# A fused attention, DFT and FFN kernel on one core: contiguous output of the first DFT stage, conversion of the second weight matrix over more slots, the first layer norm in one go, FFN at slot 37

## The chip, the cores and the metric

The kernel runs on one core of a Trainium2 chip. The metric is the time of one execution on the device in microseconds (us), as the median of several runs. A core has five engines with instruction queues of their own: TensorE (PE; its weight loads are listed as PEld), VectorE (DVE), ScalarE (ACT), GpSimd (POOL) and SyncE (SP), which here issues every DMA. Each queue runs strictly in the order in which it was written.

## The reference

```python
# attention: 8 batches, 8 heads, 512 local + 32 global tokens, head dim 64
s_ll = where(|pos_i - pos_j| <= 32, q_l @ k_l.T / 8, -1e9)
out_l = sm([q_l @ k_g.T / 8, s_ll]) @ [v_g, v_l]      # local rows: a band and the globals
out_g = sm(q_g @ [k_g, k_l].T / 8) @ [v_g, v_l]       # global rows: all keys
# x: (8, 544, 512)
mixed = real(fft(fft(x, axis=1), axis=2))
u  = x + mixed
un = (u - mean(u)) / sqrt(var(u) + 1e-6)
return u + relu(un @ w_ch1) @ w_ch2                   # 512 -> 2048 -> 512
```

The weights come as 64-bit numbers and are converted on the chip. Operands of matmuls are split into a float16 high part and a float16 low part, and each product is three matmuls: high by high, high by low, low by high.

## The kernel before, in words

`Kern.run` writes a plan: every call of a step is entered with a time, and `Plan.run` calls them in order of that time. So the plan's times are nothing but an order; each engine's queue is the order of the calls that use it. Up to time 38 (`F0`) one unit is a slot, and an attention step for 128 query rows (a "tile" u) goes in each slot; `A[u]` is u for the first 16 tiles and u + 6 afterwards (`PAUSE`: six slots without a new tile after batch 0). From `F0` on the FFN runs beside the attention: `warp` stretches the plan so that 22 slots take 32 units (two FFN chunks), and after that 2 units go to a slot.

**Attention.** Per pair of heads p: loads, scales, products by the scales, high and low parts (`prep_*`, `v_*`), then per two tiles `scores` (PE), `masked` (DVE, L409), `exps` (ACT, L418), and per tile `p_hi` (ACT, L422), `p_lo` (POOL, L426), a transposing DMA `turn`, `values` (PE, L444 and L446), and `norm` (DVE, L455 to L457). `x_out` writes the rows to a DRAM buffer `xs`; the next pair's first `norm` writes the same one-buffer tile `x`. `g_*` are the same for the global rows (`g_values`, L499). `scales` is a run of small DVE steps on two or four values a partition (L312 to L329).

**Weights.** For each of 32 tiles of 128x512 there is a load (`w_load`, 512 KB), `w_abs` (ACT, L183, into one of two PSUM buffers named ps1), and `w_bits` (four DVE passes, L191 to L194), in this order: 16 tiles of w_ch1 (k = 0), then 16 of w_ch2 (k = 1). Tile n has its `w_bits` in slot n - 8, so w_ch2 takes slots 8 to 23, one tile each. Then `w_max`, `w_fold` and `w_scale` find the scale, and `w_split` makes the two parts: for w_ch2 two ACT passes (L249, L258) and one POOL subtraction (L259). All 16 of these stand in slots 26 to 33, two to a slot. Raw tiles lie in two buffers `rw`, which share their place with the DFT's input `x4`, and in two buffers `raw`, which share theirs with the FFN's transposed input `uh`.

**DFT of a batch**, from slot R + 7 with R the batch's last tile's slot: `d_load` reads `xs`, `d_odd*` (POOL, L593 and on), `d_tail` and `d_even*` (DVE, L597 to L609 and L643 to L648) fold it, `d_hi` and `d_lo` split it. Then come five `d_first` (PE, L676 and L678; 8 matmuls of 137 columns each, the two halves of the 274 columns written to even and odd columns of a PSUM tile), each followed by `d_z` (ACT, L685) and `d_z2` (DVE, L690), which take its high and low part out of PSUM; and six `d_second` (PE, L700, 129 columns each) with `d_as`, `d_df` and `d_add`. Two steps go in a slot. Batch 0 takes its PSUM from the two buffers ps1, later ones from a single buffer psd.

**FFN**, 17 chunks of 256 rows. A chunk's layer norm (`l_stats`, `l_un`, `l_hi`, `l_lo`, `l_turn`, `l_root`; L753 to L789) starts 6 units before the chunk, 5 for chunks 0 and 1. Then for each of 8 pairs fp of blocks: `f_first` (PE, L801, 24 matmuls), `f_hi` (ACT, L806), `f_lo` (DVE, L810), and 3 units later `f_second` (PE, L820, 12 matmuls), which reads the w_ch2 tiles 2 fp and 2 fp + 1. `f_end` and `f_out` close the chunk.

Of the kernel before, what the change touches and what calls it, by code (L numbers as in the profile page):

```python
# [10 lines left out]
F16 = mybir.dt.float16  # L11
BF16 = mybir.dt.bfloat16
I32 = mybir.dt.int32
AF = mybir.ActivationFunctionType
ALU = mybir.AluOpType
# [4 lines left out]
P = 128  # L20
B, H, SL, SG, D = 8, 8, 512, 32, 64
T, DM, FF = 544, 512, 2048
NK, NL, NH = 274, 258, 129
# [4 lines left out]
NVB = 2  # L28
NKB = 2
W0 = -8  # L30
F0 = 38
PAUSE = 6
RS0 = 1.829591166069289e-20

# [40 lines left out]
class Plan:  # L75
# [3 lines left out]
    def add(self, slot, rank, fn, *a):  # L79
        self.at(self.warp(slot + rank), fn, *a)  # L80

    def at(self, time, fn, *a):
        self.q.append((time, len(self.q), fn, a))
# [6 lines left out]
class Kern:  # L90
    def __init__(self, tc, stack, ins, out):
# [57 lines left out]
        self.g, self.st, self.w, self.cur = {}, {}, {}, {}  # L149
        self.u, self.dsc, self.D, self.L, self.raw = {}, {}, {}, {}, {}  # L150

# [13 lines left out]
        return self.wd[1][i * P:(i + 1) * P, :]  # L165

    def w_load(self, k, i, n):
        if n % 4 < 2:
            if n == 0:
                rw = self.p1.tile([P, 2, 512, 2], I32, name="rw", tag="x4")  # L170
                self.rw = [rw[:, j] for j in range(2)]
            raw = self.rw[n % 2]
        else:
            raw = self.p2.tile([P, 512, 2], I32, name="raw", tag="uh")
        self.nc.sync.dma_start(raw.rearrange("p n t -> p (n t)"), self.w_src(k, i).bitcast(I32))
        self.raw[k, i] = raw
# [487 lines left out]
    def d_first(self, b, i):  # L664
        nc, d = self.nc, self.D[b]
        eh, ht = d["eh"], d["ht"]
        cs, o, d0, m = (*divmod(i, 2), 0, P) if i < 4 else (0, 0, P, 1)
        d["ps"] = ps = self.d_psum(b)[:m, 0:NK]
        base = (0, 258, 514, 770)[2 * cs + o]
        w = 128 + (base == 0)  # L670
        n = NK // 2
        for kp in (1, 0):
            c0, po = n - n * kp, ps[:, 1 - kp:NK:2]
            for k, (a, c) in enumerate(((0, 0), (0, 1), (1, 0))):
                e = base + kp * w + d0
                nc.tensor.matmul(po, eh[:, a, e:e + m], self.c1[:, cs, c, c0:c0 + n], start=k == 0, stop=False)  # L676
            e = (0, 129, 257, 385)[2 * cs + o] + d0
            nc.tensor.matmul(po, ht[:, e:e + m], self.c1t[:, cs, c0:c0 + n], start=False, stop=True)  # L678

    def d_z(self, b, i):  # L680
        d = self.D[b]
        if i < 4 and i % 2 == 0:
            d["z", i // 2] = self.p1.tile([P, 2, 2, NK], F16, name=f"z{i // 2}")
        d["hl"] = (d["z", i // 2][:, 0, i % 2], d["z", i // 2][:, 1, i % 2]) if i < 4 else (self.zr[0:1, :], self.zr[32:33, :])
        self.nc.scalar.activation(d["hl"][0], d["ps"], AF.Copy, scale=0.125)  # L685

    def d_z2(self, b, i):
        d = self.D[b]
        hi, lo = d.pop("hl")
        self.nc.vector.scalar_tensor_tensor(lo, d.pop("ps"), 0.125, hi, op0=ALU.mult, op1=ALU.subtract)  # L690

    def d_second(self, b, kt, cs):
        nc, d = self.nc, self.D[b]
# [50 lines left out]
    def l_stats(self, c):  # L744
# [3 lines left out]
        v, y = ve[:, 0], ve[:, 1]  # L748
        self.L[c] = {"mv": mv, "ve": ve, "uh": None}
        for j in range(2):  # L750
# [8 lines left out]
    def l_un(self, c, j):  # L759
        L = self.L[c]  # L760
        L["un"] = un = self.p1.tile([P, DM], F32, name="un", tag="un")
        self.nc.vector.tensor_scalar(un, self.u[c][:, j], L["mv"][:, j, 0:1], L["ve"][:, 1, j:j + 1], op0=ALU.subtract, op1=ALU.mult)  # L762

    def l_hi(self, c, j):
        L = self.L[c]
        L["hl"] = hl = self.p2.tile([P, 2, DM], F16, name="unh")
        self.nc.scalar.activation(hl[:, 0], L["un"], AF.Copy)  # L767

    def l_lo(self, c, j):
        L = self.L[c]  # L770
        self.nc.vector.tensor_sub(L["hl"][:, 1], L.pop("un"), L["hl"][:, 0])

    def l_turn(self, c, j):
        L = self.L[c]
        if j == 0:
            L["uh"] = self.p2.tile([P, 2, 8, P], F16, name="uh", tag="uh")
        self.nc.sync.dma_start_transpose(L["uh"][:, j], L.pop("hl").rearrange("p a d -> p (a d)"))

    def l_root(self, c):
        nc = self.nc  # L780
# [55 lines left out]
    def run(self):  # L836
        self.h = {}
        late = F0 + 16 + PAUSE

        def warp(t):  # L840
            if t < F0:
                return t
            return F0 + 32 * (t - F0) / (16 + PAUSE) if t < late else F0 + 32 + 2 * (t - late)

        plan = Plan(warp)
        add, at = plan.add, plan.at
# [3 lines left out]
        for n in range(32):  # L850
            k, t = divmod(n, 16)
            i = t if k else 4 * (t % 4) + t // 4
            s = W0 + n
            add(s - 3, .08, self.w_load, k, i, n)
            add(s - 1, .71, self.w_abs, k, i)
            add(s, .40, self.w_bits, k, i)
            if n % 4 == 3 and k == 0:
                c = n // 4
                add(s, .41, self.w_max, 0, c)
                add(s + 1, .62, self.w_fold)  # L860
                add(s + 2, .62, self.w_scale, 0, c)
                for kt in range(4):
                    add(s + 3 + kt, .75, self.w_split, 0, 4 * kt + c)
        s = W0 + 31
        add(s, .41, self.w_max, 1, 0)
        add(s + 1, .62, self.w_fold)
        add(s + 2, .62, self.w_scale, 1, 0)
        for f in range(16):
            add(s + 3 + f // 2, .75, self.w_split, 1, f)
        add(8, .09, self.load_consts)  # L870

        for b in range(B):
# [7 lines left out]
        for p in range(32):  # L880
# [19 lines left out]
            for half in range(2):  # L900
                t = A[4 * p + 2 * half]
# [21 lines left out]
        for b in range(B):  # L923
# [17 lines left out]
            for n, e in enumerate(steps):  # L941
                t, r = R + 14 + n // 2, (.50, .52, .56) if n % 2 == 0 else (.90, .92, .94)
# [13 lines left out]
            add(t + 2, .07, self.d_rest, b)  # L956
        at(F0 + 32 * 7 + 4.5, self.l_load)
        for c in range(17):
            F = F0 + 16 * c
            L = F - (6 if c > 1 else 5)  # L960
            at(L + .42, self.l_stats, c)
            for j in range(2):
                at(L + j + 1.425, self.l_un, c, j)
                at(L + j + 1.76, self.l_hi, c, j)
                at(L + j + 1.79, self.l_lo, c, j)
                at(L + j + 2.03, self.l_turn, c, j)
            at(L + 3.43, self.l_root, c)
            for fp in range(8):
                t = F + 2 * fp
                at(t + .30, self.f_first, c, fp)  # L970
                at(t + .54, self.f_hi, c, fp)
                at(t + .65, self.f_lo, c, fp)
                at(t + 3.30, self.f_second, c, fp)
            for j in range(2):
                at(F + 17.82, self.f_end, c, j)
            at(F + 18.04, self.f_out, c)
# [52 lines left out]
```

## Time and profile before

| | us |
|---|---|
| median of three runs | 1208.02 |
| the three runs | 1207.30, 1208.02, 1210.46 |
| the profiled execution | 1210.44 |
| its span, first to last instruction | 1208.7 |
| mean granted TensorE clock in it | 0.966 |
| first FFN matmul starts | 245.3 |

Times in views of the trace count from the first instruction. A row of busy times by stretch reads: stretch, its length, then for PE, PEld, DVE, ACT and POOL the busy time in it (and the instructions), then the granted clock, the DMA engines' busy share and GB/s. A row of the chain of waits reads: start, length, engine, tile, line, number of instructions in a row; it follows the work that ended last back to what released it. A group row reads: busy time, mean ns of one | idle time before it.

### The profile page before, as it was taken

What the parts mean: (1) busy time and instruction counts of PE and PEld (TensorE: products, weight loads), DVE (VectorE), ACT (ScalarE), POOL (GpSimd) and SP (SyncE); (2) the same over time, 40 slices, a digit from 0 to 9 for tenths busy, and PEclk for the clock granted to TensorE, in tenths of its full rate; (3) what the DMA queues carried; (4) which work ended last, traced back from release to release, by engine and by line L of the source; (5) the groups of instructions that cost most, each with busy time, mean ns of one, the idle gap of its engine ahead of it and who ended that gap; (6) DMA issues with size and microseconds to landing.
All of it is one profiled execution on the core that took longest, in us unless ns stands there. A gap on an engine that the chain in (4) does not pass through costs nothing.

```text
span 1208.7 us, 24459 instructions
## 1 busy us (share of the span) xinstructions
PE 1011.3 (84%) x9415; PEld 728.0 (60%) x9415; DVE 761.5 (63%) x2121; ACT 608.6 (50%) x1348; POOL 505.6 (42%) x473
## 2 busy tenths in 40 slices
PE   0244325499798999999999999999999999999996
PEld 0234224366575667766777677767677767666664
DVE  6998873856857575767576747674867446433221
ACT  4667569666565555665565556555554212111110
POOL 2779177745544534453446344634462311100000
PEclk9999998589898999999999999999999999999998
DMA  7669925556455645464556546644444221110000
GB/s 250 151 171 234 268 65 111 124 124 166 104 141 98 157 99 133 99 160 110 120 114 150 113 114 122 143 114 104 108 110 103 66 85 36 38 56 18 27 27 18
DMA packets 249564, 137.55 MB, mean 114 GB/s; under 512 B 200576, under 2 KB 223200, under 8 KB 249448
## 3 DMA queue, kind: packets, MB, share of 16 engines
q1 hardware_dynamic: 249448, 136.01, 46.5%
q8 instruction: 73, 1.20, 0.4%
q14 instruction: 43, 0.35, 0.1%
HBM read 65.10 MB, written 18.35 MB: 69 GB/s over the span
## 4 chain that ended last, share of the span: by engine, by line
PE 63%; DVE 24%; ACT 7%; POOL 2%; issue 2%; DMA 2%; DVEq 0%; ACTq 0%; POOLq 0%
PE acc L820 25%; PE ps L801 25%; PE S L399 3%; DVE pe L409 2%; PE psd L676 2%; PE bk L499 2%; DVE ps L192 2%; DVE ps L193 2%; DVE ps L191 2%; DVE wm L194 1%; PE psd L700 1%; PE bk L444 1%; PE bk L446 1%; DVE h L810 1%; ACT pe L418 1%
## 5 line engine op out<-in xcount | busy, mean ns | idle before, releaser
L801 PE MATMUL ps<-uh,wh 128*128 128x256 f16 x3264 | 383.2, 274 | 0.0
L820 PE MATMUL acc<-wh,h 128*128 128x512 f16 x1632 | 380.8, 384 | 0.0
L801 PEld LDWEIGHTS <-wh 128*128 128x128 f16 x3264 | 320.2, 99 | 59.6 <-issue 0.8
L810 DVE SCALAR_TENSOR_TENSOR h<-ps,h 128x512 f16<-128x512 f32 x136 | 93.7, 689 | 303.4 <-ACT h L806 303.3
L820 PEld LDWEIGHTS <-h 128*128 128x128 f16 x1632 | 154.8, 99 | 172.8 <-issue 11.5
L426 POOL TENSOR_TENSOR ph<-pe,ph 128x448 f16<-128x448 f32 x128 | 134.6, 1052 | 292.8 <-ACT ph L422 116.8
L806 ACT ACTIVATE h<-ps 128x512 f16<-128x512 f32 x136 | 80.3, 590 | 258.3 <-PE ps L801 258.1
L418 ACT ACTIVATE pe<-pe,nm 128x224 f32<-128x224 f32 x256 | 102.1, 470 | 97.9 <-DVE nm L409 97.7
L444 PE MATMUL bk<-vN,pl 128*128 128x65 f16 x768 | 74.3, 205 | 68.4 <-DVE xg L509 35.0
L409 DVE CUSTOM_DVE_ANT_0 pe<-S,msk,z 128x224 f32<-128x224 f32 x256 | 99.6, 445 | 3.1 <-PE S L399 3.1
L446 PEld LDWEIGHTS <-pl 96*128 96x128 f16 x768 | 61.5, 106 | 52.2 <-issue 50.9
L444 PEld LDWEIGHTS <-pl 128*128 128x128 f16 x768 | 64.3, 106 | 26.4 <-DMA pl<-ph 20.3
L399 PE MATMUL S<-kT,qT 64*128 64x192 f16 x768 | 57.5, 277 | 18.8 <-ACT pg L480 18.5
L422 ACT ACTIVATE ph<-pe 128x448 f16<-128x448 f32 x128 | 72.0, 563 | 0.0
L399 PEld LDWEIGHTS <-qT 64*128 64x128 f16 x1536 | 55.4, 103 | 22.5 <-issue 19.0
L377 POOL TENSOR_TENSOR kT<-qk,kT 128x512 f16<-128x512 f32 x32 | 40.8, 1274 | 53.3 <-ACT kT L372 51.4
L767 ACT ACTIVATE unh<-un 128x512 f16<-128x512 f32 x34 | 21.3, 625 | 75.4 <-DVE un L762 75.4
L446 PE MATMUL bk<-vB,pl 96*128 96x65 f16 x576 | 55.7, 205 | 0.0
L362 ACT ACTIVATE qk<-qk,z 128x512 f32<-128x512 f32 x64 | 45.5, 710 | 15.5 <-DVE z L323 15.5
L352 POOL TENSOR_TENSOR vN<-vf,vN 128x640 f16<-128x640 f32 x32 | 46.2, 1444 | 0.3 <-ACT vN L348 0.3
L593 POOL TENSOR_TENSOR s<-x 128x1020 f32<-128x1020 f32 x8 | 19.1, 2382 | 57.7 <-DMA x<-xs 30.7
L377 POOL TENSOR_TENSOR qT<-qk,qT 128x512 f16<-128x512 f32 x32 | 38.6, 1207 | 9.9 <-DMA u<-xs 6.6
(185 smaller groups left out, 1663.2 us busy)
## 6 DMA issues: line engine op xcount, KB each, us to landing
qk<-in_qk SPq DMA_DIRECT2D x32, 512.0 KB
vf<-in_v SPq DMA_DIRECT2D x32, 320.0 KB
rw<-in_moe_w_ch SPq DMA_DIRECT2D x16, 512.0 KB
raw<-in_moe_w_ch SPq DMA_DIRECT2D x16, 512.0 KB
xs<-x SPq DMA_DIRECT2D x32, 256.0 KB
out<-u SPq DMA_DIRECT2D x16, 512.0 KB
x<-xs SPq DMA_DIRECT2D x24, 256.0 KB
u<-xs SPq DMA_DIRECT2D x24, 256.0 KB
```

Of the source, the lines that this page charges most:

```text
L377: self.nc.gpsimd.tensor_sub(lo, s.pop(nm), hi)
L399: nc.tensor.matmul(ps, qT[r, a, j], k, start=m == 0, stop=m == 2)
L409: nc.vector.tensor_tensor_reduce(self.per[(4 * p + j) % 4][:, h, 0:224], S[:, h, 224 * n:224 * n + 224], self.msk[:, j], z[:, 8:9], 3e38, ...
L418: nc.scalar.activation(pe[:, h, 0:224], pe[:, h, 0:224], AF.Exp, bias=nm[:, n, h:h + 1], scale=-1.0)
L422: self.nc.scalar.activation(ph[:, 0, :, 0:224], self.per[i % 4][:, :, 0:224], AF.Copy)
L426: self.nc.gpsimd.tensor_sub(ph[:, 1, :, 0:224], self.per[i % 4][:, :, 0:224], ph[:, 0, :, 0:224])
L444: nc.tensor.matmul(pv[:, j % 2, h], pl[:, 4 * a + 2 * h], vN[:, j, c, h, :], start=m == 0, stop=False)
L446: nc.tensor.matmul(pv[:, j % 2, h], pl[0:96, 4 * a + 2 * h + 1], vb, start=False, stop=m == 2)
L801: nc.tensor.matmul(ps[:, q], wt[:, w, c0:c0 + P], uh[:, :, 4 * a + kt, :], start=n == 0, stop=n == 11)
L806: self.nc.scalar.activation(h[:, 0], self.fps, AF.Relu)
L810: self.nc.vector.scalar_tensor_tensor(h[:, 1], self.fps, 0.0, h[:, 0], op0=ALU.max, op1=ALU.subtract)
L820: nc.tensor.matmul(self.acc_f[j], h[:, a, q, j * P:(j + 1) * P], self.w[1, f][:, w, :], start=f == 0 and a == 0 and w == 0, stop=f == 15 a ...
```

## The change

Five edits.

1. `d_first` writes its two halves side by side in PSUM. `d_z` and `d_z2` read the halves as they lie and write their float16 results to every second column, so that the tiles read by `d_second` are as before.
2. The w_ch2 tile t has its `w_bits` in slot 8 + (3t // 2) where it was 8 + t: 8, 9, 11, 12, 14, 15, 17, 18, 20, 21, 23, 24, 26, 27, 29, 30. Its load and `w_abs` stay three slots and one slot ahead. `w_max`, `w_fold` and `w_scale` follow in slots 30 to 32.
3. `w_split` of w_ch2 goes to slots 33 to 48, one each (at .75), where it was 26 to 33, two each.
4. The tiles from n = 24 on no longer use `rw`: every third of them uses a new buffer `rx`, the others `raw`.
5. `F0` is 37. Chunk 0's norm is started at F0 - 4 with its halves close together (times 33.42 to 34.10, root at 36.43); it was spread over 33.42 to 36.43. Chunk 1's norm starts 6 units ahead as the later ones do (5 before). The high and low tile `hl` of a half is kept under the half's own key, since both halves are now in flight.

```diff
-F0 = 38
+F0 = 37
...
-        if n % 4 < 2:
+        if n > 23 and n % 3 == 2:
+            raw = self.p1.tile([P, 512, 2], I32, name="rx")
+        elif n < 24 and n % 4 < 2:
...
-            c0, po = n - n * kp, ps[:, 1 - kp:NK:2]
+            c0 = n - n * kp
+            po = ps[:, c0:c0 + n]
...
-        self.nc.scalar.activation(d["hl"][0], d["ps"], AF.Copy, scale=0.125)
+        self.nc.scalar.activation(self.woven(d["hl"][0]), self.halves(d["ps"]), AF.Copy, scale=0.125)
+
+    def woven(self, t):
+        return t.rearrange("p (k o) -> p o k", o=2)
+
+    def halves(self, t):
+        return t.rearrange("p (o k) -> p o k", o=2)
...
-        self.nc.vector.scalar_tensor_tensor(lo, d.pop("ps"), 0.125, hi, op0=ALU.mult, op1=ALU.subtract)
+        self.nc.vector.scalar_tensor_tensor(self.woven(lo), self.halves(d.pop("ps")), 0.125, self.woven(hi), op0=ALU.mult, op1=ALU.subtract)
...
-            s = W0 + n
+            s = W0 + (n if k == 0 else 16 + 3 * t // 2)
...
-        s = W0 + 31
...
-            add(s + 3 + f // 2, .75, self.w_split, 1, f)
+            add(s + 3 + f, .75, self.w_split, 1, f)
...
-            L = F - (6 if c > 1 else 5)
+            if c == 0:
+                L, x, y, z = F - 4, (.50, .60), (.02, .06), (.30, .50)
+            else:
+                L, x, y, z = F - 6, (1.425, 2.425), (.335, .365), (.605, .605)
             at(L + .42, self.l_stats, c)
             for j in range(2):
-                at(L + j + 1.425, self.l_un, c, j)
-                at(L + j + 1.76, self.l_hi, c, j)
-                at(L + j + 1.79, self.l_lo, c, j)
-                at(L + j + 2.03, self.l_turn, c, j)
+                at(L + x[j], self.l_un, c, j)
+                at(L + x[j] + y[0], self.l_hi, c, j)
+                at(L + x[j] + y[1], self.l_lo, c, j)
+                at(L + x[j] + z[j], self.l_turn, c, j)
```

More of the change, by code (lines that the diff above doesn't have):

```diff
@@ L765, in l_hi @@
         L = self.L[c]
-        L["hl"] = hl = self.p2.tile([P, 2, DM], F16, name="unh")
+        L["hl", j] = hl = self.p2.tile([P, 2, DM], F16, name="unh")
         self.nc.scalar.activation(hl[:, 0], L["un"], AF.Copy)
@@ L770, in l_lo @@
         L = self.L[c]
-        self.nc.vector.tensor_sub(L["hl"][:, 1], L.pop("un"), L["hl"][:, 0])
+        self.nc.vector.tensor_sub(L["hl", j][:, 1], L.pop("un"), L["hl", j][:, 0])
     def l_turn(self, c, j):
@@ L776, in l_turn @@
             L["uh"] = self.p2.tile([P, 2, 8, P], F16, name="uh", tag="uh")
-        self.nc.sync.dma_start_transpose(L["uh"][:, j], L.pop("hl").rearrange("p a d -> p (a d)"))
+        self.nc.sync.dma_start_transpose(L["uh"][:, j], L.pop(("hl", j)).rearrange("p a d -> p (a d)"))
     def l_root(self, c):
```

## The prediction

> **What bounds the kernel now.** I read the page first, then the busy times by stretch, cut where the limit changes, then the chain of waits inside the stretches that the change touches.
>
> ```profile
> PE 1011.3 (84%) x9415; PEld 728.0 (60%) x9415; DVE 761.5 (63%) x2121; ACT 608.6 (50%) x1348; POOL 505.6 (42%) x473
> PE 63%; DVE 24%; ACT 7%; POOL 2%; issue 2%; DMA 2%; DVEq 0%; ACTq 0%; POOLq 0%
> ```
>
> The first row is an average over stages that have nothing in common; the second already says that one engine (DVE) holds a quarter of the chain although it is busy less than PE.
>
> ```profile
> 80.00:119.00 39.00, 20.20 (x241) 16.45 (x241) 34.99 (x104) 29.68 (x66) 35.95 (x36) 1.00 1.01 239
> 119.00:151.50 32.50, 10.08 (x111) 8.38 (x110) 29.21 (x81) 17.50 (x41) 7.68 (x7) 1.00 0.95 262
> 151.50:170.00 18.50, 3.68 (x37) 3.50 (x39) 15.91 (x35) 7.69 (x22) 15.21 (x12) 1.00 0.29 63
> 170.00:210.00 40.00, 19.58 (x228) 16.58 (x225) 17.78 (x63) 39.46 (x79) 28.80 (x28) 0.90 0.48 104
> 210.00:245.30 35.30, 17.09 (x199) 14.28 (x199) 30.21 (x81) 22.73 (x50) 24.60 (x25) 0.55 0.57 126
> 245.30:306.70 61.40, 57.44 (x614) 41.83 (x613) 38.47 (x122) 42.88 (x103) 35.13 (x31) 0.96 0.56 137
> 306.70:388.10 81.40, 70.15 (x697) 51.31 (x692) 57.17 (x165) 45.18 (x106) 36.76 (x37) 0.92 0.49 110
> 450.70:570.50 119.80, 116.21 (x1143) 83.54 (x1141) 80.31 (x235) 68.54 (x157) 55.82 (x51) 0.99 0.53 123
> ```
>
> These are slots 8 to 15, slots 16 to 23, the front of batch 0's DFT, the slots of the w_ch2 splits, the way to the FFN, FFN chunks 0 and 1, and one later batch with its two chunks. Four regimes: DVE (with POOL beside it in the first row) up to 151.5; ACT at 39.46 of 40 from 170; DVE at 30.21 of 35.3 up to the first FFN matmul; PE afterwards. So there are two currencies. Before 245.3 a microsecond counts only if it is taken from the engine named; from then on it counts if PE is spared it.
>
> **The change part by part.**
>
> *1. DFT stage one.* In the PE-bound part the chain shows what a matmul costs there, start to start:
>
> ```profile
> 445.15 0.35 PE psd L676 x3
> 445.50 0.12 PE psd L678
> 445.61 0.35 PE psd L676 x3
> 445.96 0.12 PE psd L678
> ...
> 349.14 0.34 PE psd L700 x6
> ```
>
> ```profile
> L676 PE MATMUL psd<-c1r,eh 128*128 128x137 f16 x168 | 27.5, 315 | 0.5 <-DVE z L690 0.5
> L676 PE MATMUL psd<-c1r,eh 128*1 128x137 f16 x42 | 6.8, 314 | 0.0
> ```
>
> Four matmuls of 137 columns take 0.35 + 0.12 = 0.47, or 0.117 each; six of 129 columns with contiguous output take 0.34, or 0.057 each. The columns differ by 6%, the price by a factor of two. The last two rows exclude the weights: with 128 weight columns or one the matmul is as long (315 and 314 ns). What is left is the output to every second column, which the change removes. Contiguous I take 0.057 x 137/129 = 0.060, so 0.057 is saved per matmul, 40 matmuls a batch: 2.3 a batch. Batches 2 to 7 lie where PE is the bound, as the row from 450.7 shows (116.21 of 119.8): all of it. Batch 1 lies in 306.7 to 388.1, where PE has 11 of idle time: half. Batch 0 lies before the FFN, where PE is not the bound: nothing. 6.5 x 2.3 = **14.9**; ends 11.5 (five batches) and 16.1 (seven).
>
> The Trainium skill, page "SBUF — State Buffer", section "Door 1: The DMA port swizzle", says that PSUM is accessed in 8-byte lines and that non-contiguous patterns slow matmuls down significantly; the 0.117 against 0.057 agrees. By its page "TensorE: Matmul & The Clock Gate", section "Wait — 56ns, not 53.3ns?" (columns over 2.4 GHz plus 2.5 ns), 137 columns take 0.0596, an estimate with which the term would be the same.
>
> The stride moves to the readers, and the trace has no float16 write to every second column. Nearest rows:
>
> ```profile
> L690 DVE SCALAR_TENSOR_TENSOR z<-psd,z x28: 431/443/444, 330.5 to 1031.5; 128x274 f16<-128x274 f32 x28
> L685 ACT ACTIVATE z<-psd 128x274 f16<-128x274 f32 x28 | 11.0, 394 | 39.9 <-PE psd L678 39.5
> L716 DVE SCALAR_TENSOR_TENSOR asm<-psd,dsc,asm 128x258 f32<-128x258 f32 x14 | 6.7, 478 | 5.6 <-PE psd L700 2.9 <-PE bk L446 2.7
> L727 DVE TENSOR_TENSOR u<-u,asm 128x255 f32<-128x255 f32 x16 | 16.2, 1012 | 0.0
> ```
>
> L716 writes f32 to every second column: 478 for 258, which is 508 for 274 against L690's 443, so +0.065, or 0.3 a batch. The far end is L727, which runs backwards over two SBUF inputs: 1.01. Then a reader would lose 0.6, two readers 1.2 per step; steps are half a slot apart, and a slot of a batch is 119.8 / 16 = 7.5, so PE's other work still hides it, except in batch 0 (5 x 1.2 = 6). I take L716: 0.
>
> *2. Slots 8 to 23: five `w_bits` tiles fewer* (11 instead of 16).
>
> ```profile
> 140.41 0.69 DVE L191 TENSOR_SCALAR_CACHE_REDUCE ps<-ps 128x512 f32<-128x512 f32 x1
> ...
> 143.26 0.69 DVE L191 TENSOR_SCALAR_CACHE_REDUCE ps<-ps 128x512 f32<-128x512 f32 x1
> ```
>
> A tile costs DVE 2.85 from one L191 to the next. Two leave slots 8 to 15, but there POOL is busy 35.95 of 39 and gives up nothing: at most 3, I take 2. Three leave slots 16 to 23, where all else is far from busy: 8.5, of which I take 7, because the last pair's `norm` waits for a DMA as well:
>
> ```profile
> 126.66 6.03 DMA xs<-x
> ```
>
> With fewer 512 KB loads on SP's queue and the DMA engines (share 0.95) that transfer starts earlier, but its 6 stay. **9**; ends 4 and 14 (5 x 2.85).
>
> *3. Slots 24 to 37.* The five tiles return here, at 24, 26, 27, 29 and 30, and 12 of 16 splits leave for slots 37 to 48.
>
> ```profile
> L249 ACT ACTIVATE wh<-wm,wsc 128x512 f16<-128x512 f32 x32 | 22.7, 709 | 0.0
> L258 ACT ACTIVATE wm<-wm,wsc 128x512 f32<-128x512 f32 x16 | 11.5, 722 | 0.5
> L259 POOL TENSOR_TENSOR wh<-wm,wh 128x512 f16<-128x512 f32 x32 | 36.8, 1154 | 11.4 <-ACT wm L258 9.9 <-DMA qk<-in_qk 0.2
> L183 ACT ACTIVATE ps<-rw 128x512 f32<-128x512 f32 x16 | 10.0, 622 | 15.0 <-DVE wm L194 8.1 <-DMA rw<-in_moe_w_ch 6.7
> ```
>
> Balance over 151.5 to 245.3 (93.8): ACT 69.9 - 12 x 1.36 (0.71 + 0.72 less overlap) + 5 x 0.62 = 56.7; POOL 68.6 - 12 x 1.15 = 54.8; DVE 63.9 + 14.3 = 78.2; PE 40.4. DVE becomes the bound everywhere, and 78 is a floor: at most 16 can go, 18 if DVE's own steps shorten. By stretch: 151.5 to 170, already DVE's, takes two tiles (5.7) and loses `w_max` to `w_scale` (3): +2.5. 170 to 210 loses the ACT bound: DVE's 17.78, three tiles (8.5) and 2 of `w_max` make 28, and with waits on ACT's `eh` and PE's `d_first` I take 31: -9. `w_bits` of the last tile holds a ps1 buffer, so `d_first` 2 waits for it on PE with `scores` behind it; that is in the 31. 210 to 245.3 is DVE's, and part of its time is not work:
>
> ```profile
> 170.26 0.16 DVE L325 SCALAR_TENSOR_TENSOR z<-z 128x2 f32<-128x2 f32 x1
> ...
> 222.89 1.07 DVE L325 SCALAR_TENSOR_TENSOR z<-z 128x2 f32<-128x2 f32 x1
> ...
> 237.57 0.69 DVE L771 TENSOR_TENSOR unh<-un,unh 128x512 f16<-128x512 f32 x1 [1.97 <-ACT unh L767]
> ```
>
> The same step on two elements takes 0.16 alone and 1.07 while POOL subtracts. Of the splits there, two at 33.75 become one and the two at 32.75 go, under the norm's small steps (some 1.5 less blocking); with the norm's halves close together the 1.97 wait goes (halves and root cost DVE the same). The norm's two transposes pass SP's transposes of two tiles, whose `p_lo` is ready later anyway: 0. So -3.5. Sum 2.5 - 9 - 3.5 = **-10**; ends -3 and -18.
>
> *4. FFN at 37.* The chain's last steps ahead of the first FFN matmul:
>
> ```profile
> 242.74 0.21 PE bk L444
> ...
> 243.55 1.76 PE bk L499 x15
> 245.32 0.75 PE ps L801 x3
> ```
>
> ```profile
> 344.85 0.98 PE bk L499 x15
> ...
> 1191.75 2.62 PE ps L801 x24
> 1194.37 5.19 PE acc L820 x24
> ```
>
> `f_first` now stands ahead of `values` (L444) and `g_values` (L499): it starts 2.6 earlier. PE does them afterwards, where L499 takes 0.98 instead of 1.76 and L444's part shrinks as much, so 1.4 comes back: **-1**; ends 0 and -3. The slot's PE work beside it is only moved. (A pair fp of the FFN takes 2.62 + 5.19 / 2 = 5.2.)
>
> *5. Chunk 0 with 11 splits.* ACT 42.88 + 11 x 1.36 = 57.8 of 61.4, POOL 47.8, PE 57.44. ACT stands as near its limit as PE, and `f_hi`, `exps` and `p_hi` queue behind each split (1.36). PSUM's two buffers and 3 units between `f_first` and `f_second` hide one such delay, not queues of them: **+4**; ends 0 and 10. The last split (48.75) precedes its reader (48.89) by 0.14 slot, 0.8 at 61.4 / 11 a slot, against 1.36 + 1.15 of work: one PE wait of 2 to 3, which is in the 4.
>
> *6. Chunk 1's norm 0.7 slot sooner.*
>
> ```profile
> 300.32 1.22 DVE x L597
> ...
> 305.09 1.20 DVE ve L783
> ...
> 308.79 1.09 DVE ve L786
> ```
>
> Its root ran among the DFT's folding, at 1.1 to 1.2 a step. Now it is ahead of it: **-1.5**; ends 0 and -4. `rx` is one more buffer, and the `raw` tiles end slots before `uh` is written: 0.
>
> Sum: -14.9 - 9 - 10 - 1 + 4 - 1.5 = -32.4 on the profiled 1210.44: 1178. The median of the runs is 2.4 lower than that execution; I predict **1177**.
>
> **The rivals.**
>
> *Chunk 0 pays back (14%).* ACT at 94% with waits on PE and DVE in between cannot run full, and half of the twelve splits end on the path: +16 instead of +4, 1189. For it: the 170 to 210 row, in which ACT at 99% set the pace. Against: there were two splits a slot, now one. The Trainium skill, page "SBUF — State Buffer", section "Who interferes with whom", says that a DVE step with two SBUF inputs is blocked while POOL reads SBUF; it speaks against the change, since 11 subtractions now meet chunk 0's DVE steps, and by it 11 x 1.15 = 12.7 of DVE delay is an upper estimate. L325's rows agree with the blocking.
>
> *DVE is no faster before the FFN (13%).* The tiles meet the fold where DVE and POOL block each other (151.5 to 170: DVE 15.91, POOL 15.21 of 18.5), and parts 2 and 3 bring 5 instead of 19: 1191.
>
> *The matmuls stay at 0.117 (6%).* Were it another cause, part 1 gives 0: 1192. L700 and the one-column rows speak against it.
>
> *Slower (4%).* `f_second` of pair fp stands at 39.27 + 1.375 fp, its later split at 34.75 + 2 fp. If ACT lags PE by two slots in chunk 0, the last four pairs all wait, PE idles in each, and its clock falls as in 210 to 245.3 (0.55). ACT's stretch took 40 for 12 splits, six slots, so 6.7 a slot: at that pace 11 slots take 73, +12. Half clock on the chunk's eight pairs of 5.2 adds up to 42. Against -36.4 of the other parts it becomes slower once two thirds of the chunk run so (+28): 1214, at most 1228. Against it: in chunk 0 ACT now has 18 idle.
>
> **How the numbers follow.** Forecast 63%, the rivals as given. The ends of the parts add up to 1155 and 1202; they won't all fall together. Below I stop at 1162, above at 1194, which takes in three rivals' centres. A measurement of this kernel tells about 0.3% (3.6 us) from no change. Each of the first three rivals alone is still faster; the first two together (1203 and up) are the 0.03 within 0.3%; the last is the 0.04 slower; 0.93 is left for faster.
>
> **What would show it.** Right: L676 start to start 0.06 in the chain and d_first pairs at 0.5; first FFN matmul at 220 to 227; ACT below 85% and DVE above 85% in the slots of batch 0's DFT; chunk 0 between 61 and 68 long; later batches 117.5 instead of 119.8. Wrong: `acc` matmuls of chunk 0 released by POOL's `wh`, first FFN matmul after 235, or L690 above 0.6.

## The result, and the profile after

The changed kernel takes 1222.93 us (median of four runs, 1221.58 to 1224.25), the kernel before beside it 1209.24 (four runs, 1207.30 to 1210.46). The ratio is 1.0115, with a 95% interval of 1.0093 to 1.0136: 13.7 us slower, where 32 faster was predicted. The predicted range, 1162 to 1194, does not hold it, and none of the rivals gives it by its own mechanism. A few executions took half again to three times as long as the others of their kernel (one of 3443.28, of a kernel further down, is the one that was profiled), and all times and ratios here leave them out.

The first FFN matmul did come earlier, by 19.2 where 21.6 was forecast. The span, cut at the same events in three kernels (the third is the first experiment, the change with only `F0` put back to 38), shows where it was lost:

| stretch, us | before | after | change with F0 = 38 |
|---|---|---|---|
| up to the first FFN matmul | 245.3 | 226.1 | 229.7 |
| FFN chunk 0 | 61.4 | 67.9 | 70.9 |
| FFN chunk 1 | 81.4 | 79.5 | 77.2 |
| FFN chunks 2 to 11 | 592.0 | 622.2 | 576.6 |
| chunk 12 to the end | 228.6 | 226.4 | 226.3 |
| span | 1208.7 | 1222.1 | 1180.7 |

At the start of chunk 2 the changed kernel is still 14.6 ahead (373.5 against 388.1). It then loses 30.2 in ten chunks (622.2 less 592.0) that the prediction expected to shorten by 2.3 a batch.

The page of the kernel after, busy shares and then the chain of waits by engine:

```profile
PE 1009.4 (83%) x9415; PEld 716.2 (59%) x9415; DVE 743.7 (61%) x2121; ACT 610.6 (50%) x1348; POOL 507.4 (42%) x473
PE 57%; DVE 25%; ACT 8%; POOL 3%; DMA 3%; issue 3%; SPq 0%; DVEq 0%; POOLq 0%; ACTq 0%
```

PE's share of the chain fell from 63% to 57%: PE waits more, although its matmuls became cheaper. The busy times by stretch of the kernel after (stretch, length, then PE, PEld, DVE, ACT and POOL busy, granted clock, DMA share, GB/s), for batch 0's DFT, the way to the FFN, chunks 0 and 1, and a later pair of chunks:

```profile
166.00:198.00 32.00, 18.99 (x207) 15.52 (x207) 26.07 (x80) 23.37 (x54) 17.85 (x17) 0.85 0.61 138
198.00:226.10 28.10, 13.67 (x172) 11.14 (x171) 23.03 (x78) 19.41 (x43) 17.04 (x17) 0.56 0.51 127
...
226.10:294.00 67.90, 59.52 (x607) 42.40 (x603) 37.70 (x130) 54.32 (x118) 46.05 (x42) 0.93 0.63 136
294.00:373.50 79.50, 68.25 (x714) 48.39 (x714) 56.52 (x157) 50.59 (x115) 43.04 (x42) 0.93 0.50 112
438.40:564.70 126.30, 116.79 (x1141) 82.70 (x1140) 79.00 (x235) 68.75 (x157) 56.65 (x51) 0.96 0.53 116
```

A pair of chunks, which is one batch, takes 126.3 where it took 119.8. PE is busy 116.79 of it against 116.21, and idle for 9.5 against 3.6. The waits of PE in a later pair say for what. First the kernel after, chunks 4 and 5 (501.1 to 627.3; in all, times, longest):

```profile
PE bk L446 <- DMA plg<-pgr: 6.3, 1, 6.3
PE bk L446 <- DVE xg L511: 2.1, 1, 2.1
PE bk L568 <- DVE zv L314: 1.0, 1, 1.0
PE bk L446 <- DVE x L459: 0.2, 1, 0.2
```

Then the same chunks before (510.1 to 629.9; L444 and L509 there are L446 and L511 after):

```profile
PE bk L444 <- DVE xg L509: 2.6, 1, 2.6
PE bk L566 <- DVE zv L312: 1.0, 1, 1.0
```

Two things are new. The longest wait of chunk 4 has grown from 2.6 to 6.3, and chunk 5, in which PE waited for nothing, has one of 2.1 for `xg`, the normalised output of the global rows. Both come in the pairs of chunks 2, 4, 6 and 8; chunk 10 has one of 5.2 and chunk 11 none. The name `plg` (the transposed probabilities of the global rows) on the 6.3 misleads: only `g_values` (L501) reads that tile, and L446 is the next `values`. `values` and `g_values` write the same PSUM tile `bk`, out of which `xg` is read, and `xg` ends at 558.19 where L446 starts at 558.24. In the kernel before and in the change with `F0` = 38, whose waits are put down to `xg` by name, the same matmul also starts 0.05 after its end. So PE waits for `xg`, and the DMA only lands at the same moment. The chain of waits of the kernel after, around this wait:

```profile
545.95 0.36 DVE pe L411
546.32 0.47 DVE un L771
...
547.35 1.46 ACT pe L420 x4
...
550.59 0.49 ACT h L815
551.10 0.69 DVE h L819
551.79 1.14 DVE unh L780
552.94 1.66 DVE eh L638
...
555.64 2.61 DMA plg<-pgr
558.25 0.20 PE bk L446
...
560.29 4.54 PE acc L829 x12
...
567.46 0.18 PE psd L679 x3
```

L771 and L780 are the norm of a later chunk, and they now stand right behind `masked` (L411). The norm's halves wait for ACT, which first does its own queue (L420 to L815). DVE's `eh` and `ht` (parts of the next batch's DFT), the `scales` and `xg` wait behind the norm; in the kernel before, as in the change with `F0` at 38, they stand ahead of it. DVE's own rows of the stretch show where it stands idle (in brackets: for how long, and for whom):

```profile
547.48 0.69 DVE L780 TENSOR_TENSOR unh<-un,unh 128x512 f16<-128x512 f32 x1 [0.70 <-ACT unh L776]
...
551.10 0.69 DVE L819 SCALAR_TENSOR_TENSOR h<-ps,h 128x512 f16<-128x512 f32 x1 [2.35 <-ACT h L815]
...
557.85 0.34 DVE L511 TENSOR_SCALAR xg<-bk,dng 64x128 f32<-64x128 f32 x1
```

The same place in the chain of the change with `F0` = 38:

```profile
533.54 0.36 DVE pe L411
533.91 0.62 DVE bst L762
...
538.56 1.12 DVE eh L638
...
542.24 0.35 DVE xg L511
...
542.64 0.21 PE bk L446
...
544.69 3.31 PE acc L829 x12
```

From the last L411 to the PE matmul it is 12.3 in the one (545.95 to 558.25) and 9.1 in the other (533.54 to 542.64): 3.2 more, about what the longest wait grows by, from 2.6 to 6.3. DVE is idle in it for 0.70 + 2.35 = 3.05 in the one and not at all in the other, and has about as much work in both (9.3 and 9.1), so the loss in this stretch is time in which DVE waits for ACT. ACT is late because the norm's high part (L776) now stands ahead of the exponentials (L420) on its queue and needs `un` (L771), which DVE computes behind all of `masked`: L420 starts 2.6 after the first `masked` step (544.76 to 547.35), with `F0` at 38 only 0.5 (532.35 to 532.89).

### The profile page after: what moved, and what is told of

It is laid out like the page before. It is cut to its first block, busy times and chain, and to the rows that moved or that the text cites. A ratio compares the mean times of both kernels' runs of the same rounds, so it can differ in the third digit from the quotient of the medians.

```text
span 1222.1 us, 24477 instructions
## 1 busy us (share of the span) xinstructions
PE 1009.4 (83%) x9415; PEld 716.2 (59%) x9415; DVE 743.7 (61%) x2121; ACT 610.6 (50%) x1348; POOL 507.4 (42%) x473
## 4 chain that ended last, share of the span: by engine, by line
PE 57%; DVE 25%; ACT 8%; POOL 3%; DMA 3%; issue 3%; SPq 0%; DVEq 0%; POOLq 0%; ACTq 0%
PE acc L829 24%; PE ps L810 23%; PE S L401 3%; DVE pe L411 2%; ACT pe L420 2%; DVE ps L195 1%; ACT h L815 1%; DVE ps L194 1%; DVE wm L196 1%; PE bk L501 1%; PE bk L446 1%; DVE ps L193 1%; PE psd L709 1%; DVE h L819 1%; DVE unh L780 1%
## 5 line engine op out<-in xcount | busy, mean ns | idle before, releaser
L829 PE MATMUL acc<-wh,h 128*128 128x512 f16 x1632 | 389.9, 390 | 6.1 <-POOL wh L261 3.2
L815 ACT ACTIVATE h<-ps 128x512 f16<-128x512 f32 x136 | 80.7, 593 | 280.4 <-PE ps L810 275.7
L446 PE MATMUL bk<-vN,pl 128*128 128x65 f16 x768 | 74.9, 206 | 88.1 <-DVE xg L511 31.2
L420 ACT ACTIVATE pe<-pe,nm 128x224 f32<-128x224 f32 x256 | 101.9, 469 | 88.2 <-DVE nm L411 88.1
L411 DVE CUSTOM_DVE_ANT_0 pe<-S,msk,z 128x224 f32<-128x224 f32 x256 | 99.7, 445 | 3.8 <-POOL kT L379 2.8
L446 PEld LDWEIGHTS <-pl 128*128 128x128 f16 x768 | 64.6, 106 | 22.1 <-DMA pl<-ph 16.3
L401 PE MATMUL S<-kT,qT 64*128 64x192 f16 x768 | 60.1, 286 | 17.6 <-ACT pg L482 17.2
L776 ACT ACTIVATE unh<-un 128x512 f16<-128x512 f32 x34 | 21.2, 624 | 67.7 <-DVE un L771 67.7
L261 POOL TENSOR_TENSOR wh<-wm,wh 128x512 f16<-128x512 f32 x32 | 37.1, 1158 | 24.4 <-ACT wm L260 22.3
L343 POOL TENSOR_TENSOR vf<-vf,zv 128x640 f32<-128x640 f32 x32 | 45.2, 1413 | 2.2 <-DVE zv L314 2.2
```

The costliest lines, as they stand in the source:

```text
L401: nc.tensor.matmul(ps, qT[r, a, j], k, start=m == 0, stop=m == 2)
L411: nc.vector.tensor_tensor_reduce(self.per[(4 * p + j) % 4][:, h, 0:224], S[:, h, 224 * n:224 * n + 224], self.msk[:, j], z[:, 8:9], 3e38, ...
L420: nc.scalar.activation(pe[:, h, 0:224], pe[:, h, 0:224], AF.Exp, bias=nm[:, n, h:h + 1], scale=-1.0)
L446: nc.tensor.matmul(pv[:, j % 2, h], pl[:, 4 * a + 2 * h], vN[:, j, c, h, :], start=m == 0, stop=False)
L815: self.nc.scalar.activation(h[:, 0], self.fps, AF.Relu)
L829: nc.tensor.matmul(self.acc_f[j], h[:, a, q, j * P:(j + 1) * P], self.w[1, f][:, w, :], start=f == 0 and a == 0 and w == 0, stop=f == 15 a ...
```

## The experiments

**Is it the F0 edit?** Two kernels, one edit each way.

```diff
 # the change, F0 put back; chunk 0's norm keeps its slots
-F0 = 37
+F0 = 38
...
-                L, x, y, z = F - 4, (.50, .60), (.02, .06), (.30, .50)
+                L, x, y, z = F - 5, (.50, .60), (.02, .06), (.30, .50)
```

> The changed kernel with F0 back at 38; chunk 0's norm keeps its slots, all other edits stay. Theory P (phase): with F0 at 37 each later chunk's norm falls one slot earlier against the attention, into the slot whose masked step serves two tiles and ahead of the transposes of the pair's tiles, and this costs about 9 us a batch. Then a pair of later chunks takes 117 to 118 us here (126.3 in the changed kernel, 119.8 before), the first FFN matmul starts about one slot later (230 to 234), and the total is about 1185. Rival R (readers): the strided reads and writes of d_z and d_z2, or another edit that acts in every batch, cost it; then a pair of chunks stays near 126 and the total is 1220 to 1226.

Measured: 1182.44 us (1181.67 to 1186.10), ratio to before 0.9793 (0.9761 to 0.9824); a pair takes 117.4 (496.0 to 613.4). The edit, taken alone on the kernel before:

```diff
-F0 = 38
+F0 = 37
...
-            L = F - (6 if c > 1 else 5)
+            L = F - (6 if c > 1 else 4 + c)
```

> The kernel before with F0 at 37 alone (chunk 0's norm then starts 4 units ahead, which keeps its slots; chunk 1's 5 ahead as before). Theory P: a pair of later chunks takes about 128.6 us (119.8 + 8.8), the total is about 1245. Rival R: a pair stays at 119.8, the total is 1203 to 1208.

Measured: 1245.20 us (1244.88 to 1248.36), ratio 1.0312 (1.0281 to 1.0343). Its first FFN matmul comes 3.3 earlier (242.0), a pair takes 127.1 (513.6 to 640.7), and the waits of PE in it hold the same two rows:

```profile
PE bk L444 <- DMA plg<-pgr: 6.3, 1, 6.3
PE bk L444 <- DVE xg L509: 2.0, 1, 2.0
```

So "FFN at slot 37" costs 3.1% on the kernel before and 3.3% on the changed one (1.0115 / 0.9793), some 38 to 40 us (1245.20 less 1207.17, 1222.93 less 1182.44), and all the rest of the change together gains 2.1%.

**Which queue, and is it the norm at all?** With F0 = 37 everything of a later chunk stands one slot earlier against the attention: the norm, and the FFN's own steps. Five kernels move the norm or a part of it. First, the norm another slot earlier:

```diff
-                L, x, y, z = F - 6, (1.425, 2.425), (.335, .365), (.605, .605)
+                L, x, y, z = F - (8 if c > 2 else 6), (1.425, 2.425), (.335, .365), (.605, .605)
```

> The changed kernel with the norm of chunks 3 and on started 8 units ahead instead of 6, one slot earlier, so that its halves fall in the slots without a masked step again. Theory P in the form that the slot of the norm is what matters: a pair of later chunks takes 118 to 120 us, the total is about 1190. Rival C: the place of the chunk's own start and end against the attention is what matters (f_first, f_end); then a pair stays near 126 and the total near 1222.

Measured: 1205.29 us (1202.64 to 1208.20), ratio 0.9976 (0.9956 to 0.9997), a pair 121.7 (494.6 to 616.3). Not quite half of the loss goes: the wait of 6.3 is gone, but in this pair 2.9 for `xg` (two waits, the longer 2.2) and 1.8 for ACT's `pg` (L482) stand in its place. That is between the two expectations.

Second, only the SP queue: `plg` is transposed on the queue on which the norm's `uh` transposes now stand ahead of it.

```diff
-                L, x, y, z = F - 6, (1.425, 2.425), (.335, .365), (.605, .605)
+                L, x, y, z = F - 6, (1.425, 2.425), (.335, .365), (.605, .605) if c < 2 else (2.595, 1.605)
```

> The changed kernel with only SP's order altered: from chunk 2 on the two transposes of the norm (uh) are issued after the pair's transposes (pl of slot 42, plg of 42.005) instead of ahead of them; DVE, ACT and POOL keep their order. Theory Q: SP's queue alone is the cause; the 6.3 us wait of PE for plg in the even chunk goes, and with it the half clock behind it; a pair of later chunks takes 118 to 120 us, total about 1190. If DVE's and ACT's order in that slot is the cause too, the odd chunk's stall (PE waits for DVE xg) stays: a pair at 122 to 124, total 1205 to 1212. If SP's order is not a cause: 126, 1222.

Measured: 1222.05 us (1218.24 to 1223.97), ratio 1.0111 (1.0077 to 1.0145), as the change. The wait of PE only changes its name; chunks 5 and 6 of this kernel:

```profile
PE bk L446 <- DVE xg L511: 8.3, 2, 6.3
...
```

With `plg` issued ahead of the norm's transposes, the same 6.3 is put down to `xg`, which stands behind the norm in both. SP's order is not the cause, as the third expectation had it.

Third, the norm in the slots that it had in the kernel before, with the FFN at 37:

```diff
-                L, x, y, z = F - 6, (1.425, 2.425), (.335, .365), (.605, .605)
+                L, x, y, z = F - (4 if c > 1 else 6), (1.425, 2.425), (.335, .365), (.605, .605)
```

> The changed kernel (F0 at 37) with the norm of chunks 2 and on started 4 units ahead instead of 6: against the attention the norm is then in exactly the slots of the kernel before, while the chunk's own matmuls stay one slot earlier. Theory N (the place of the norm's DVE and ACT steps in the attention's order is the cause): a pair of later chunks takes 117 to 118 us, total about 1180. Rival C (the place of the chunk's matmuls, f_hi, f_lo or f_end against the attention): a pair stays near 126, total near 1222. The transposed rows are now ready only some 2 us ahead of the chunk; if that is too late, each chunk waits for them and a pair takes 119 to 122.

Measured: 1240.92 us (1239.03 to 1241.88), ratio 1.0270 (1.0240 to 1.0299), a pair 126.2 (504.3 to 630.5): slower still, above every total that was expected. The pair is as long as the second expectation had it, but the waits are those of the third, at more than its price. The waits of PE in chunks 4 and 5:

```profile
PE ps L810 <- DMA uh<-unh: 6.1, 2, 4.3
PE bk L446 <- DVE xg L511: 2.6, 1, 2.6
...
```

`xg` is back at its 2.6 of before, as the norm's place would have it. But the FFN's input `uh` now comes late by 6.1 a pair, 4.3 of it in one wait. The wait has moved from one side of the norm to the other. Most of the further 18 over the change lie behind the attention: chunk 12 to the end takes 239.4 instead of 226.4.

Fourth, the test that separates the norm from the FFN's own steps: F0 = 38, where a pair takes 117.4, and only the norm moved into the slots that the change gives it.

```diff
 # on the change with F0 = 38
-                L, x, y, z = F - 6, (1.425, 2.425), (.335, .365), (.605, .605)
+                L, x, y, z = F - (8 if c > 1 else 6), (1.425, 2.425), (.335, .365), (.605, .605)
```

> The change with F0 = 38, and from chunk 2 on only the layer norm one slot earlier: its halves then stand in the slots in which the change has them (right behind masked, ahead of eh, ht, z and xg), while the FFN's matmuls stay where the fast version has them. Theory N (the norm's place in the DVE and ACT queues costs the 8.8 us a batch): the wait for the global rows' transposed tile comes back, a pair of chunks takes 123 to 126, 1215 to 1235 us. Rival M (the place of the FFN's own matmuls and of their ACT and DVE steps against the attention costs it): a pair stays at 117 to 118, 1180 to 1187 us.

Measured: 1221.75 us (1220.04 to 1223.30), ratio 1.0121 (1.0091 to 1.0150). The FFN's matmuls stand where the change with `F0` = 38 has them, and the loss is there in full: 39.3 over the 1182.44. Chunks 2 to 11 take 616.7 (375.5 to 992.2) against 576.6. The waits of PE from 500 to 630, the upper two rows:

```profile
PE bk L446 <- DMA plg<-pgr: 6.3, 1, 6.3
PE bk L446 <- DVE xg L511: 2.1, 1, 2.1
```

Fifth, between the two places, half a slot later than the change has it:

```diff
-                L, x, y, z = F - 6, (1.425, 2.425), (.335, .365), (.605, .605)
+                L, x, y, z = F - (5 if c > 1 else 6), (1.425, 2.425), (.335, .365), (.605, .605)
```

> The change, and from chunk 2 on the norm's halves half a slot later (one unit). Theory T (at F0 = 37 no place is left: early, the norm delays the global rows' tile by 6.3 us; at its old slots the transposed input of the FFN comes 4.3 us late): half a slot is 3.7 us, so the late input shrinks to about 0.6 and the delay of the global rows' tile mostly goes: a pair 119 to 123, 1190 to 1210 us. Rival M (the place of the FFN's own matmuls costs it, wherever the norm is): 125 to 127 a pair, 1215 to 1225 us.

Measured: 1202.60 us (1200.04 to 1205.58), ratio 0.9961 (0.9944 to 0.9979), a pair 121.8 (498.5 to 620.3), as the first expectation had it. Both waits are there, smaller (500 to 630):

```profile
PE bk L446 <- DVE xg L511: 5.3, 2, 4.4
...
PE ps L810 <- DMA uh<-unh: 0.6, 1, 0.6
```

The five together: in this order of the attention the norm needs a place behind `xg` on DVE, and from there more time before the FFN's first matmul than `F0` = 37 leaves it. At 38 it has both, at 37 none of the four places that were tried has both. No run moves the norm's DVE steps without its ACT step, so the part of each is read from the trace alone: the 3.05 of DVE idle time above is a wait of each queue for the other.

**Can the earlier start be kept?** The first two chunks are the stretch in which the plan gives 32 units to 22 slots. With 23 slots for them the FFN starts at 37 and every later chunk stands as with F0 = 38.

```diff
-        late = F0 + 16 + PAUSE
+        late = F0 + 17 + PAUSE
...
-            return F0 + 32 * (t - F0) / (16 + PAUSE) if t < late else F0 + 32 + 2 * (t - late)
+            return F0 + 32 * (t - F0) / (17 + PAUSE) if t < late else F0 + 32 + 2 * (t - late)
```

> The changed kernel with F0 at 37 for chunks 0 and 1 alone: they are spread over 23 slots instead of 22, so that chunk 2 and all later ones stand where they stood with F0 at 38. Theory P: a pair of later chunks takes 117.6 us as in the run with F0 at 38; the first FFN matmul starts at 226 as in the changed kernel; the total is 1178 to 1183, at or a little under that run, because PE has idle time in the first two chunks. If the first two chunks only stretch by what the start gains, the total is 1182 to 1186.

Measured: 1178.90 us (1178.36 to 1179.34), ratio 0.9757 (0.9725 to 0.9789): faster than the kernel before and than the change. Its median is 3.5 under that of the change with F0 = 38, but the two intervals overlap. The first FFN matmul is at 226.7, chunks 0 and 1 take 70.5 and 77.0, chunks 2 to 11 576.8. The page's chain row is back at before's share of PE:

```profile
PE 63%; DVE 20%; ACT 8%; POOL 4%; issue 3%; DMA 2%; SPq 0%; DVEq 0%; POOLq 0%; ACTq 0%
```

**What are the other parts worth?** Only the contiguous first stage of the DFT, on the kernel before:

```diff
-            c0, po = n - n * kp, ps[:, 1 - kp:NK:2]
+            c0 = n - n * kp
+            po = ps[:, c0:c0 + n]
 # and d_z, d_z2 with woven() and halves(), as in the change
```

> The kernel before with the contiguous output of the first DFT stage alone. The predicted term: 2.3 us less in each later pair of chunks (117.5), 14.9 in all: total about 1193. If the readers' strides (ACT 481 ns instead of 394, DVE 470 instead of 441 in the changed kernel) take some of it back: 1195 to 1200.

Measured: 1191.46 us (1189.55 to 1192.39) against 1206.71, ratio 0.9860 (0.9832 to 0.9888); a pair 117.7 (446.3 to 564.0). The first expectation is the nearer one.

Only the w_ch2 tiles' `w_bits` and splits over more slots (with the buffer `rx`), F0 = 38, norms as before:

```diff
-            s = W0 + n
+            s = W0 + (n if k == 0 else 16 + 3 * t // 2)
...
-            add(s + 3 + f // 2, .75, self.w_split, 1, f)
+            add(s + 3 + f, .75, self.w_split, 1, f)
```

> The kernel before with the w_ch2 edit alone (w_bits and splits over more slots, the buffer rx), F0 at 38. The predicted terms 2, 3 and 5: first FFN matmul at 229 to 234 (245.3 before), chunks 0 and 1 together 146 to 150 (142.8 before), total 1207 - 13 + 5, about 1198. Rival: nothing is gained ahead of the FFN without the first norm in one go (first FFN matmul after 240) and the total is 1207 to 1214.

Measured: 1201.29 us (1200.87 to 1205.08), ratio 0.9947 (0.9926 to 0.9969). The first FFN matmul is at 236.0, 9.3 earlier, between the two expectations; chunk 0 takes 67.0, 5.6 longer, and the total is 3 above the first expectation.

On the change with F0 = 38, the splits two a slot again, behind the spread tiles:

```diff
-            add(s + 3 + f, .75, self.w_split, 1, f)
+            add(s + 3 + f // 2, .75, self.w_split, 1, f)
```

> The change with F0 = 38 and the w_ch2 splits two a slot again (slots 33 to 40 instead of 33 to 48), 1182.44 us with them spread. By the prediction's parts 3 and 5 the spread takes about 10 ahead of the FFN and gives 4 back in chunk 0: here the first FFN matmul comes 4 to 8 later than 229.7, chunk 0 is 2 to 5 shorter than 71.0, 1185 to 1189 us. Rival (the last splits are late in chunk 0, so that the spread gives back all that it brings): 1176 to 1183 us.

Measured: 1185.35 us (1184.12 to 1187.60), ratio 0.9822 (0.9794 to 0.9850). The median lies in the first expectation, but the intervals of this kernel and of the one with the splits spread (0.9761 to 0.9824) overlap, and the stretches are not as expected: the first FFN matmul is at 230.2 instead of 229.7, not 4 to 8 later, and chunk 0 is longer, 76.1, not shorter. A miss for the reasoning in both directions. Chunks 0 and 1 together take 149.0, against 148.1 with the splits spread.

On the change with F0 = 38, the norms of chunks 0 and 1 as before:

```diff
-            if c == 0:
-                L, x, y, z = F - 5, (.50, .60), (.02, .06), (.30, .50)
-            else:
-                L, x, y, z = F - 6, (1.425, 2.425), (.335, .365), (.605, .605)
+            if True:
+                L, x, y, z = F - (6 if c > 1 else 5), (1.425, 2.425), (.335, .365), (.605, .605)
```

> The change with F0 = 38 and the norms of chunks 0 and 1 as before, 1182.44 us with the new ones. By the prediction's parts 3 and 6 the norm in one go is worth 2 and chunk 1's earlier norm 1.5: 1184 to 1187 us, the first FFN matmul 2 later than 229.7. Rival (neither is on the path): 1181 to 1183.5 us.

Measured: 1189.88 us (three runs, 1186.81 to 1190.70), ratio 0.9851 (0.9817 to 0.9885). This is the kernel of the 3443.28, and no stretch of it is read. By the medians the new norms are worth 7 (1189.88 less 1182.44), twice the 3.5 of the prediction, though its interval and that of the change with F0 = 38 (0.9761 to 0.9824) just overlap.

## Why the prediction was wrong

**The step that failed is part 4**, "FFN at 37", and in it the sentence "The slot's PE work beside it is only moved". It priced one event, the first FFN matmul of chunk 0, at -1 with ends 0 and -3. But F0 is the origin of all chunks. The edit moved the norm of each later chunk by a slot against the attention, past `eh` and `ht` of the next DFT, the `scales` and `xg` on DVE, and past ACT's exponentials. In the ten chunks from 2 to 11 that costs 45.6 (622.2 against 576.6), and 38 to 40 in the whole time, which the runs with the edit alone and without it show from both sides, and the run at F0 = 38 with only the norm moved shows that the norm is what does it. The trace of before had the warning: the longest releaser of idle time on L444 was `xg`. PE's matmuls by line, before:

```profile
L444 PE MATMUL bk<-vN,pl 128*128 128x65 f16 x768 | 74.3, 205 | 68.4 <-DVE xg L509 35.0 <-DVE x L457 23.7 <-DMA pl<-ph 3.5
```

(The last figures are PE's idle time ahead of the line, and for whom.) Later pairs had 3.6 of idle time, of which 2.6 were this one wait: it was already the tightest point of a batch. The question "what stands behind the norm on DVE" was asked for chunks 0 and 1 (parts 3 and 6) and not for the others.

The two waits cost 8.9 a pair, more than they last, since PE's clock fell with them. Busy times by stretch of the kernel after, around the 6.3 (PE's matmuls ahead of the gap end at 551.97, those behind it start at 558.24), and behind that:

```profile
...
550.00:556.00 6.00, 1.97 (x19) 1.61 (x17) 4.88 (x4) 3.15 (x7) 5.39 (x4) 1.00 0.36 81
556.00:560.30 4.30, 2.06 (x37) 1.85 (x37) 3.71 (x23) 0.72 (x1) 0.00 (x0) 0.64 0.32 75
560.30:564.80 4.50, 4.50 (x14) 1.68 (x15) 3.26 (x13) 2.06 (x5) 0.05 (x1) 0.59 0.93 146
```

The granted clock is 1.00 up to 556, 0.64 over the end of the gap and 0.59 behind it, and the twelve `acc` matmuls take 4.54 there; in the chain of the change with F0 = 38 they take 3.31. That kernel's pair:

```profile
496.00:613.40 117.40, 113.82 (x1141) 81.50 (x1140) 79.70 (x236) 68.54 (x159) 55.78 (x52) 0.99 0.55 125
```

Against it the idle time grows by 5.9 (3.7 in the even chunk's wait, 2.1 in the odd one's) and the busy time, at the lower clock, by 3.0.

**Part 1 was right** in mechanism, and in size with some luck: 14.9 predicted; the medians of the kernel with this edit alone differ by 15.2, and its ratio gives 13.5 to 20.3 of 1206.7. The groups of the kernel after, by form:

```profile
L679 PE MATMUL psd<-c1r,eh 128*128 128x137 f16 x168 | 16.5, 223 | 0.0
L688 ACT ACTIVATE z<-psd 128x274 f16<-128x274 f32 x28 | 13.5, 481 | 29.3 <-PE psd L681 29.3
L699 DVE SCALAR_TENSOR_TENSOR z<-psd,z 128x274 f16<-128x274 f32 x28 | 13.2, 470 | 17.7 <-ACT z L688 17.7
```

The matmul's mean falls from 315 to 223 ns; in the chain, quoted above, three L679 take 0.18, so 0.06 each, as forecast. The readers pay: ACT 481 instead of 394, and DVE 470 instead of 443, less than the 508 that the nearest row gave. They are hidden as said: with this edit alone a pair shortens by 2.1, against 2.3. But by stretches chunks 2 to 11 shorten by 15.3 (592.0 to 576.7), where five batches at 2.3 make 11.5. Part of the surplus is PE's clock: in the kernel before it was low behind each of the four waits of 2.6 for `xg`, with this edit alone behind two of the four, and the prediction had no term for that.

**Parts 2, 3 and the norm of chunk 0** have the right sum by chance of two errors. The first FFN matmul was forecast between 220 and 227 and came at 226.1; 9 + 10 + 2.6 = 21.6 earlier was the sum, 19.2 came. Inside it, the tiles and splits bring 9.3 (the kernel with them alone), where 9 and 10 less the norm's 2 make 17, and the norm in one go, taken at 2, brings most of the rest: from 236.0 to 229.7 is 6.3, and the DFT edit alone does not bring the start forward (247.0). This 6.3 is a difference between two kernels, not an experiment with the norm alone. The edit of `F0` brings 3.6 (229.7 to 226.1), 2.6 forecast. That ACT would give up the bound was right: 73% in 166 to 198 and 69% behind it. DVE is the busiest at 81% and 82%, under the 85 that was named, so waits between the engines remain, and they are probably what parts 2 and 3 left too small.

**Part 5** was +4 with ends 0 and 10. Chunk 0 became 6.5 longer in the change, 5.6 with the spread alone, 9.5 at F0 = 38: in the range, on its upper side. Of the two mechanisms named, the queue behind ACT's splits is in the waits of F0 = 38, and the late last split in those of the change, which the prediction also gave as a sign of being wrong (`acc` released by POOL's `wh`). But the last split's waits stand at 301.2 and 304.5, behind the start of chunk 1 (294.0), and so are no part of the 6.5. In chunk 0 itself PE of the change waits 8.5 (2.9 for `zv`, 2.5 for `pg`, 2.4 for `x`, 0.7 for `nm`) against 3.8 before, and is busy for 2.1 more. PE's waits around the end of chunk 0, after (283 to 311):

```profile
PE acc L829 <- POOL wh L261: 3.2, 1, 3.2
PE acc L829 <- ACT wh L251: 2.8, 1, 2.8
```

And over chunk 0 with F0 = 38 (229.7 to 300.6):

```profile
PE S L401 <- ACT pg L482: 12.1, 2, 8.7
```

The last split was priced as one wait of 2 to 3 and makes two, 6.0 together. In chunk 0 with F0 = 38 PE waits 12.1 for ACT's `pg` where it waited 3.5 before, while ACT is busy 58.42 of 70.9: `pg` stands in ACT's queue behind splits (L251, L260) and the squares for the next pairs' scales (L311). So the mechanism of the rival "Chunk 0 pays back" is there, at 9.5 of its 16. Why two splits a slot make chunk 0 longer still (76.1) stays open: PE's wait for `pg` in it is no longer than with one a slot (11.9 against 12.1), but it also waits 2.4 for `x` and 1.2 for `nm`, and is busy for 2.1 more.

**Part 6** and the DFT of batch 1 were 1.5 and 1.2 in chunk 1; it is 1.9 shorter in the change and 4.2 at F0 = 38, and no run takes the two apart.

The sum of the parts gives 1178 for the profiled execution and so 1175.6 for the median, where the prediction wrote 1177; the slip changes nothing here. Without part 4 the sum was -31.4. The change with F0 = 38 is 24.7 under its own before in the medians (1182.44, 1207.17), a ratio of -1.8 to -2.4%, which is 21 to 29. So the other five parts together were some 2 to 10 too optimistic, and the one edit that was priced by a single event turned the sign: the later batches, whose 117.5 the prediction named as a sign of being right, take 126.3 with it and 117.4 without. The rival "Slower" had the sign but not the cause: it put the loss into chunk 0, with `f_second` behind late splits, and chunk 0 is 67.9, not the 89 that it needed.

## What to carry to other kernels

Where an order is written out by hand against an origin, moving the origin is one edit for each repetition: list, for every step that moves, which instructions it passes on each engine's queue, in the steady part and not only at the first use, and multiply by the number of repetitions. A stage with little slack (here 3.6 of 119.8, most of it one wait) is where a step put ahead of the releaser costs its whole delay, and here half as much again by the clock. And the name that a wait bears in a profile can be that of an event that only ended with it: ask whether the waiting instruction reads or overwrites that tile at all, and whether the wait stays as long when that event is moved away.

## What the hardware showed that was not expected

A short gap can cost PE clock, and need not. In the change with F0 = 38 PE idles 2.6 for `xg`; the busy times by stretch around it:

```profile
...
540.00:542.60 2.60, 0.04 (x1) 0.00 (x0) 2.33 (x13) 0.00 (x0) 0.00 (x0) 0.98 0.05 11
542.60:544.70 2.10, 2.06 (x37) 1.86 (x37) 1.37 (x3) 1.63 (x4) 0.00 (x0) 0.50 0.00 0
544.70:548.00 3.30, 3.30 (x14) 1.40 (x15) 2.54 (x6) 1.70 (x4) 1.04 (x1) 0.82 0.38 84
```

The granted clock is 0.50 behind a gap of 2.6, for 2.1 and part of the next 3.3. The same wait of 2.6 comes in the next batches too. The first 3.40 behind it in this batch and in the next, of the same kernel:

```profile
542.64:546.04 3.40, 3.40 (x40) 2.33 (x40) 2.33 (x4) 2.97 (x6) 1.04 (x1) 0.52 0.13 29
659.97:663.37 3.40, 3.40 (x47) 2.13 (x47) 2.33 (x4) 2.96 (x6) 1.04 (x1) 1.00 0.13 29
```

Of this kernel's four such gaps two are followed by a low clock (0.71 and 0.52) and two by 1.00; in the kernel before all four are (0.63 to 0.51), and in the kernel after so are the four gaps of 2.1 in the odd chunks (0.53 or 0.54). What decides it, no run here shows. The Trainium skill, page "TensorE: Matmul & The Clock Gate", section "Why this matters for your kernels", advises no idle gaps over about 3 us between bursts of matmuls; here gaps under that were enough in some batches, so the measurement decides. The gap of 6.3 leaves the clock low for longer (0.64 and 0.59 over 8.8).

Writing float16 results to every second column costs ACT 87 ns on 128x274 (394 to 481) and DVE, which also reads the high part in that order, 27 (443 to 470). The PSUM write to every second column that it replaces cost TensorE about half of its rate: 0.117 a matmul, now 0.06.
